# Moving the FFN weight loads from head 0 to head 3, and the gate matrix from eight DMA engines to four

## The chip, the cores and the metric

The kernel runs on one core of a Trainium2 chip. The metric is the device time of one execution in microseconds (us). Kernels are compared by the ratio to the runs of the kernel before taken in the same rounds on the same chip.

Three words are used throughout. A core's loads are carried out by sixteen *DMA engines*; a large load is cut into sixteen parts, and each part adds one to a semaphore when it has landed. A *packet* is one record of one DMA engine's work in the trace. *Delay* of an engine is how much later its last part landed than it would have with none of the extra work discussed here.

## The reference

A decode step for one token: layer norm of a row of 448 values, attention of 16 query heads over 8 cached heads of 65,536 keys of 256 values, and a small gated FFN, all added up. The cache is 512 MB in bf16 and each byte is used once; the FFN weights are three matrices of 1.6 MB.

```python
x = A_x;  xn = layernorm(x)
q = (xn @ wq)                         # 16 heads of 256
p = softmax(q @ k_cache^T / 16)       # 65536 keys in each of 8 cached heads
o = (p @ v_cache) @ wo
r = xn @ w_r
y = (silu(xn @ w_gate) * (xn @ w_up)) @ w_down
out = x + o + xn + y * sigmoid(r)     # one token: the top-1 choice is that token
```

## The kernel before

One queue (SyncE) issues all loads in a fixed order into a ring of buffers; an item is overwritten when TensorE has freed it. K and V items are 4 MB each, so every part is eight packets of 32 KB. V items of head h alternate with K items of head h+1.

```python
SPREAD = True

def flat_dma(src, n, off, spread):
    def d(a):
        dst = a[:, off:off + RP * n // 2]          # 128 partitions
        v = src.rearrange("a b -> (a b)")
        if spread:                                 # outer dim 8: eight DMA engines
            return dst, v.rearrange("(u a n) -> a u n", a=8, u=P // 8)
        return dst, v.rearrange("(p n) -> p n", p=P)
    return d
...
def v_next():
    ...
    kv_item(*v)
    if v[2] == 0 and v[3] == 2 * V_CHUNKS[0]:      # head 0, after its third V item
        item("ffn1", RP * F, [flat_dma(B_w_gate, F, 0, SPREAD), flat_dma(B_w_up, F, RP * F // 2, False)])
    if v[2] == 0 and v[3] == 3 * V_CHUNKS[0]:
        item("ffn2", FK * D, [... B_w_down ...])
...
def prog_sp():                                     # the queue that issues
    for n, it in enumerate(items):
        for m in range(max(0, it["need"] - 8), it["need"] + 1):
            wait("sp", "pe", ("FREE", m))
        for d in it["dmas"]:
            dst, src = d(ap_of(n))
            nc.sync.dma_start(dst, src).then_inc(sem_it[it["sem"]], 16)
```

In the regrouped view of the gate matrix, partition 16a+u of the buffer gets block 8u+a of the matrix (128 blocks of 12,544 bytes). TensorE's side gets a permuted copy of the input row for it, so the arithmetic is right either way. The up matrix is loaded plainly: partition p gets block p.

## Time and profile before

| | before |
|---|---|
| time | 1312.2 us (median) |
| bytes read, mean rate | 549 MB, 419 GB/s |
| PE busy | 70% |
| DMA share in the chain of waits | 73% |
| rate in a usual slice | 430 GB/s |
| rate in slices 5 and 6 (131 to 197 us) | 384 and 335 GB/s |

First the page of the kernel before: the parts with the span in 40 slices (DMA busy share in tenths, and what the engines moved), the queues, and the chain of waits.

```profile
DMA  9999999999999999999999999999999999999994
GB/s 400 430 430 430 384 335 433 431 427 432 431 430 429 429 430 429 431 429 431 431 431 431 428 430 430 431 430 429 428 430 429 431 423 430 430 430 431 431 430 205
...
q1 hardware_dynamic: 22026, 549.04, 98.5%
q8 instruction: 75, 1.23, 0.4%
q14 instruction: 12, 0.10, 0.0%
...
DMA 73%; PE 26%; another core or an unknown queue 1%; SPq 0%; issue 0%; DVE 0%
```

The engines never rest, and the rate is flat except for one dip. The dip is not idleness: the DMA share stays at 9. The windows view of the same kernel shows that (length, busy times, clock; the last two columns are DMA share and rate):

```profile
100.00:130.00 30.00, 27.56 (x304) 21.13 (x301) 20.38 (x36) 18.04 (x25) 0.00 (x0) 0.94 1.00 430
157.00:178.50 21.50, 8.88 (x112) 6.12 (x110) 5.66 (x9) 6.10 (x7) 0.00 (x0) 0.81 1.00 222
```

For 21.5 us sixteen busy engines moved 222 GB/s: 21.5 x (1 - 222/430) = 10.4 us were lost. In the packet records these are the very microseconds in which gate packets are in flight. A gate packet (12,544 bytes) takes about 0.94 us; a packet of the up matrix, of the same size, takes 0.47 us once the gate is done; K packets on engines without gate work take 2.38 us (median) instead of 1.21. This is called the *slow phase* below.

A load counts as landed only when its last part has. So the next thing to look at is how far apart the sixteen parts land. These three rows are worked out from the trace's semaphore records: when the first part of a load landed, and how much later each of the sixteen did, sorted. The records do not name the engines; which part belongs to which engine is inferred here and below from the order of the parts and its changes.

```
before, first part at   offsets of the sixteen parts (us)
 147.5 (before gate)    0.0 0.1 0.2 0.3 0.4 0.5 1.0 1.1 1.5 1.6 1.6 1.9 2.2 3.1 3.3 3.6
 191.0 (after gate)     0.0 0.5 1.2 1.3 2.0 2.7 2.8 2.8 7.3 7.4 7.7 7.8 8.6 9.7 10.6 11.0
1286.2 (last load)      0.0 0.4 3.7 4.0 4.0 4.2 6.8 9.6 9.7 9.8 9.9 10.5 10.6 11.4 19.2 19.5
```

(The last load of the queue is a piece of `wo`. The last V item, two loads before it, has the same offsets within 0.2 us.)

The gate opens a gap of 7 us between the eight engines that had it and the eight that had not. Between the second and the third row, eight engines fall back by about 9 us more: these carry the instruction fetches of queue 8, which go round eight engines in turn (75 packets of 16 KB, about 1.07 us each plus a slower neighbour packet). Two engines belong to both groups; they are 19 us behind at the end. The kernel ends 5 us after they do.

### The profile page before, as it was taken

Reading aid. Unit: us, or ns where it says so; the run is one execution under the profiler, and the core shown is the slowest. Engines: PE = TensorE matmul, PEld = TensorE weight load, DVE = VectorE, ACT = ScalarE, POOL = GpSimd, SP = SyncE. Lnnn points to the kernel's source line nnn. Section 1 sums busy time; section 2 is a strip of 40 time slices with the busy share of each in tenths; the row PEclk is TensorE's granted clock in tenths of the full one; section 3 lists DMA queues with packets and bytes.
Section 4 is the critical chain, followed back from the end, with each engine's and each line's share of the span. In section 5 each row is a group of like instructions: output and inputs, shape, how many; then the busy total and the mean of one; then the engine's idle time right before and its main releaser. Section 6 shows DMA issues by size and latency. Waiting matters only on the chain.

```text
span 1310.5 us, 20912 instructions
## 1 busy us (share of the span) xinstructions
PE 922.5 (70%) x9576; PEld 694.6 (53%) x9576; DVE 539.0 (41%) x895; ACT 432.4 (33%) x559; POOL 4.5 (0%) x34
## 2 busy tenths in 40 slices
PE   4998837768668577677677677577676686786534
PEld 4886625546546456455555556455465565565201
DVE  5776404444344344344343354344343353453200
ACT  2665303333233233233233243233332342332100
POOL 1000000000000000000000000000000000000000
PEclk9999768888888788787887888888887887888756
DMA  9999999999999999999999999999999999999994
GB/s 400 430 430 430 384 335 433 431 427 432 431 430 429 429 430 429 431 429 431 431 431 431 428 430 430 431 430 429 428 430 429 431 423 430 430 430 431 431 430 205
DMA packets 22117, 550.37 MB, mean 420 GB/s; under 512 B 2315, under 2 KB 4366, under 8 KB 4878
## 3 DMA queue, kind: packets, MB, share of 16 engines
q1 hardware_dynamic: 22026, 549.04, 98.5%
q8 instruction: 75, 1.23, 0.4%
q14 instruction: 12, 0.10, 0.0%
q10 hardware_dynamic: 4, 0.00, 0.0%
HBM read 549.03 MB, written 0.00 MB: 419 GB/s over the span
## 4 chain that ended last, share of the span: by engine, by line
DMA 73%; PE 26%; another core or an unknown queue 1%; SPq 0%; issue 0%; DVE 0%
DMA ring<-in_A_k_cache_dram 66%; PE ps_t L374 18%; DMA ring<-in_A_v_cache_dram 6%; PE ps_q L401 4%; PE ps_o L694 2%; PE ps_s L434 1%; PE ps_m L579 0%; SPq L304 0%; PE ps_m L644 0%; PE ps_s L562 0%; PE ps_m L534 0%; PE ps_m L505 0%; DVE ob_sb L514 0%; DVE res_bf L547 0%
## 5 line engine op out<-in xcount | busy, mean ns | idle before, releaser
L374 PE MATMUL ps_t<-ident_f,ring 128*128 128x128 f32 x4096 | 602.3, 310 | 302.1 <-DMA ring<-in_A_k_cache_dram 300.3
L374 PEld LDWEIGHTS ps_t<-ident_f,ring 128*128 128x128 f32 x4096 | 536.2, 161 | 419.1 <-DMA ring<-in_A_k_cache_dram 328.6
L358 DVE COPY kt_buf<-ps_t 128x1024 bf16<-128x1024 bf16 x768 | 492.6, 685 | 629.7 <-PE ps_t L374 628.7
L360 ACT ACTIVATE kt_buf<-ps_t 128x1024 bf16<-128x1024 bf16 x256 | 262.1, 1024 | 430.0 <-PE ps_t L374 429.2
L386 ACT ACTIVATE s<-ps_q 98x512 bf16<-98x512 f32 x256 | 152.9, 597 | 330.2 <-PE ps_q L401 330.2
L401 PE MATMUL ps_q<-kt_buf,qT_sb 128*2 128x512 bf16 x2048 | 173.5, 417 | 0.0
L694 PE MATMUL ps_o<-ring,S_sb 128*4 128x512 bf16 x2048 | 136.0, 410 | 48.9 <-DMA ring<-in_A_v_cache_dram 46.9
L694 PEld LDWEIGHTS ps_o<-ring,S_sb 128*4 128x4 bf16 x2048 | 50.7, 88 | 121.9 <-DMA ring<-in_A_v_cache_dram 54.9
L434 PEld LDWEIGHTS ps_s<-sel_bf,s 128*128 128x128 bf16 x1024 | 67.8, 102 | 7.6 <-ACT s L386 1.6
L434 PE MATMUL ps_s<-sel_bf,s 128*128 128x8 bf16 x1024 | 64.8, 169 | 0.7 <-ACT s L386 0.7
L514 DVE CAST ob_sb<-ps_o 100x512 bf16<-100x512 f32 x8 | 5.5, 692 | 83.2 <-PE ps_o L694 83.2
L401 PEld LDWEIGHTS ps_q<-kt_buf,qT_sb 128*2 128x2 bf16 x2048 | 26.3, 79 | 5.6 <-issue 0.2
L607 PE MATMUL ps_m<-xnT_sb,ring 128*128 128x2 bf16 x210 | 8.5, 179 | 18.0 <-DMA ring<-in_B_w_up_dram 16.4
L607 PEld LDWEIGHTS ps_m<-xnT_sb,ring 128*128 128x128 bf16 x210 | 8.4, 127 | 18.6 <-DMA ring<-in_B_w_up_dram 16.9
L480 ACT ACTIVATE S_sb<-S_sb,negmax 128x512 bf16<-128x512 bf16 x16 | 13.4, 863 | 5.3 <-DVE negmax L473 5.3
L414 DVE CAST S_sb<-ps_s 128x512 bf16<-128x512 f32 x16 | 10.9, 681 | 1.3 <-PE ps_s L434 1.3
L416 DVE TENSOR_REDUCE m1p<-S_sb 128x2 f32<-128x512 bf16 x16 | 11.0, 686 | 0.6
L592 DVE TENSOR_TENSOR gs_sb<-ps_m,sg_sb 128x14 f32<-128x14 f32 x1 | 0.2, 173 | 23.9 <-ACT sg_sb L587 23.9
L708 PE MATMUL ps_m<-ident_bf,xe_row 1*128 1x1 bf16 x16 | 0.6, 161 | 12.9 <-DVE xe_row L822 12.9
L505 PEld LDWEIGHTS ps_m<-rowsum,ones_f 128*128 128x128 f32 x32 | 5.5, 246 | 6.0 <-issue 6.0
L587 ACT ACTIVATE sg_sb<-ps_m 128x14 f32<-128x14 f32 x1 | 0.2, 184 | 22.2 <-PE ps_m L607 22.2
L708 PEld LDWEIGHTS ps_m<-ident_bf,xe_row 1*128 1x128 bf16 x16 | 0.5, 100 | 12.9 <-DVE xe_row L822 12.9
(67 smaller groups left out, 73.7 us busy)
## 6 DMA issues: line engine op xcount, KB each, us to landing
ring<-in_A_k_cache_dram SPq DMA_DIRECT2D x63, 4096.0 KB, 44.1
ring<-in_A_v_cache_dram SPq DMA_DIRECT2D x63, 4096.0 KB, 37.3
ring<-in_A_wq_dram SPq DMA_DIRECT2D x1, 3584.0 KB, 11.4
ring<-in_A_wo_dram SPq DMA_DIRECT2D x8, 448.0 KB, 29.2
ring<-in_A_k_cache_dram SPq DMA_DIRECT2D x2, 1024.0 KB, 13.4
ring<-in_A_k_cache_dram SPq DMA_DIRECT2D x1, 2048.0 KB, 20.6
ring<-in_A_v_cache_dram SPq DMA_DIRECT2D x1, 2048.0 KB, 41.6
ring<-in_B_w_gate_dram SPq DMA_DIRECT2D x1, 1568.0 KB
```

The lines of the kernel that those rows point to most:

```text
L358: op(e, ("EV", g), lambda x: x.tensor_copy(out=kt[:, :], in_=tb[:, :]))
L360: op(e, ("EV", g), lambda x: x.activation(out=kt[:, :], in_=tb[:, :], func=ACTF.Copy))
L374: ins = nc.tensor.matmul(ps_tf[g % NTB][:, jj * P:(jj + 1) * P], lhsT=kv[:, j + GN * m + jj, :], rhs=ident_f[:, :], is_transpose=True, sta ...
L386: op("act", ("EVQ", s), lambda e: e.activation(out=s2[s % 2][0:QROWS, :], in_=ps_q[0:QROWS, :], func=ACTF.Copy))
L401: ins = nc.tensor.matmul(ps_q[32 * m:32 * m + rep, 0:512], lhsT=qT_sb[:, hf, h * rep:(h + 1) * rep], rhs=kt[:, :].rearrange("p (k f) -> p ...
L414: op("dve", ("SCOPY", b), lambda e: e.tensor_copy(out=S[:, k * SBN:(k + 1) * SBN, :], in_=ps_s[:, :, :]))
L416: op("dve", ("SMAX", b), lambda e: e.tensor_reduce(out=m1p[:, h % 2, :, k], in_=S[:, k * SBN:(k + 1) * SBN, :].rearrange("p n i -> p i n") ...
L434: ins = nc.tensor.matmul(o, lhsT=s2[s % 2][:, jj * P:(jj + 1) * P], rhs=sel_bf[:, :, :], start=True, stop=True)
L480: op("act", ("EXPI", h, i), lambda e, i=i: e.activation(out=S[:, :, i], in_=S[:, :, i], func=ACTF.Exp, bias=negmax[:, h, i:i + 1], scale=1 ...
L505: ins = nc.tensor.matmul(ps_m[0:P, C_TOT + f * rep:C_TOT + (f + 1) * rep], lhsT=ones_f[:, :], rhs=rowsum[:, h, :], start=True, stop=True)
L607: ins = nc.tensor.matmul(o, lhsT=cols(a, rr * width, c), rhs=X[:, x0:x0 + 2], start=(b == 0), stop=(b == RP * half - 1), skip_group_check= ...
L694: ins = nc.tensor.matmul(ps_o[32 * g:32 * g + 2 * rep, :], lhsT=S[:, k:k + 2, :].rearrange("p n i -> p (n i)"), rhs=kv[:, j:j + 2, :], sta ...
```

## The change

Intent: place the FFN loads later, and keep the gate matrix off more of the DMA engines by giving it to the lowest four. ("At head h" means: issued among the V items of head h.) Cut to its core:

```diff
-SPREAD = True
+SPREAD = 4
+FFN_AT = 3
@@ flat_dma
-                return dst, v.rearrange("(u a n) -> a u n", a=8, u=P // 8)
+                return dst, v.rearrange("(u a n) -> a u n", a=spread, u=P // spread)
@@ v_next
-        if v[2] == 0 and v[3] == 2 * V_CHUNKS[0]:
-            item("ffn1", RP * F, [flat_dma(B_w_gate, F, 0, SPREAD), flat_dma(B_w_up, F, RP * F // 2, False)])
-        if v[2] == 0 and v[3] == 3 * V_CHUNKS[0]:
+        if v[2] == FFN_AT and v[3] == 2 * V_CHUNKS[0]:
+            item("ffn1", RP * F, [flat_dma(B_w_gate, F, 0, SPREAD), flat_dma(B_w_up, F, RP * F // 2, 0)])
+        if v[2] == FFN_AT and v[3] == 3 * V_CHUNKS[0]:
@@ dve_base: waits for RES of head FFN_AT - 1
@@ prog_dve: the permuted input row follows SPREAD
-        xv8 = xn_bf[0:1, :].rearrange("o (u a s) -> o a u s", s=RP, a=4)
+        xv8 = xn_bf[0:1, :].rearrange("o (u a s) -> o a u s", s=RP, a=SPREAD // 2)
```

Instruction counts and bytes are the same in both kernels.

## The prediction

> **What bounds it now.** Data transfer, in every stage. The page gives 420 GB/s, DMA share 9 of 9 in all slices but the last, PE busy 70%; the chain of waits is 73% DMA. By the windows view a normal stage moves 430 GB/s. So the time is set by the DMA engine that finishes last.
>
> The landings of each load's sixteen parts show that the engines are not level. Parts land within 3.6 us of each other at 147 us, within 11.0 us after the FFN loads (181 us), within 19.5 us at the end (1286.2 to 1305.7). Chaining packet records by start and end, I read the causes:
> - Instruction fetches (queue 8: 75 packets of 16 KB, about 1.07 us) go round eight engines. Each costs its engine about 1.5 us, 14 us per engine in all.
> - The gate matrix lies on eight engines, 16 packets of 12.5 KB each at about 0.94 us. Up packets of the same size take 0.47 us once the gate is done.
> - While any gate packet is in flight, all sixteen engines run at half speed: in the window 157 to 178.5 us, 222 GB/s with a DMA share of 1.00; 32 KB packets take about 2.4 us instead of 1.21. That is the 384 and 335 GB/s dip of the page: 10.6 us lost by everyone.
> - Delays come to about 11 us for an engine with neither load, 18 with gate only, 25 with fetches only, 33 with both. Two engines have both, and they end the kernel; six have the gate without these fetches (two of them with fetches of queue 14, up to 4 us).
>
> **What the change does.** Bytes, instructions and matmul counts stay. (1) The FFN loads move from head 0 to head 3, about 157 to about 630 us. DMA is the limit in both places, so this alone is worth about 0; the PE work stays hidden. (2) The gate goes over four engines, 32 packets each. The Trainium skill (DMA: Bandwidth & Descriptors, "Why a DMA increments its semaphore by 16 and not by 1") says a hardware-queue load on k engines uses the lowest-numbered k. The trace agrees so far: the small x load (one packet) ran on an engine that also had the gate, and that one shows no fetch of queue 8 up to the gate. I guess that the lowest four are free of these fetches.
>
> **Cost.** If a gate packet still takes 0.94 us and halves the rest, the slow phase is 30 us instead of 21. Delays (estimates): gate engines about 30, fetch engines 15 + 14 = 29, others 15. The last engine is at about 30 instead of 33: 3 us gained, on the critical path in full. Better balance (no engine with both loads) is mostly paid for by a slow phase half as long again.
>
> **Time: 1309 us**, range 1299 to 1322. Faster by over 2%: 0.02; within 2%: 0.96; slower by over 2%: 0.02.
>
> **Right if** the dip moves to about 610 to 660 us, is about 30 us long at about 220 GB/s and costs about 15 us; no dip near 160 us; the final spread shrinks from 19.5 to about 15 us, without two engines far behind the rest; the last V part lands about 3 us earlier.
>
> **Wrong if** one of the lowest four has the fetches of queue 8: its delay is 44 us and the kernel is some 10 us slower. If the queue-14 engines are among them, the gain is gone (+1). If more partitions per engine make the conflict worse (a third of the rate), +10 us; if four streams hurt the rest less than eight, the gain could be 10 to 14 us.

## The result and the profile after

The changed kernel took 1314.99 us (median of 4 runs, 1314.2 to 1315.3) against 1312.21. The ratio is 1.0025, with a 95% interval of 1.0007 to 1.0042: the same within 2%, but on the slow side, and so not the 3 us gained that the prediction named. (A ratio is the mean time of one kernel's runs over that of the other's in the same rounds, so not quite the ratio of the medians.) Executions over 1.5% slower than the fastest of the same kernel are left out of the means.

The page of the changed kernel, the lines that answer to those above:

```profile
DMA  9999999999999999999999999999999999999995
GB/s 400 431 430 430 429 431 431 430 430 429 431 431 427 429 430 431 427 430 429 259 420 409 429 430 431 429 432 426 430 431 431 429 430 430 429 432 430 430 430 227
...
DMA 69%; PE 28%; another core or an unknown queue 2%; SPq 0%; issue 0%; DVE 0%
```

And its windows: where the dip was, where it is now, and the stretch after it.

```profile
157.00:178.50 21.50, 15.80 (x166) 11.91 (x165) 9.33 (x16) 7.10 (x10) 0.00 (x0) 0.84 1.00 429
...
627.20:660.70 33.50, 13.65 (x139) 9.24 (x137) 7.74 (x12) 7.30 (x9) 0.00 (x0) 0.70 1.00 254
...
656.80:659.90 3.10, 0.00 (x0) 0.00 (x0) 0.00 (x0) 0.00 (x0) 0.00 (x0) 0.50 0.94 344
...
660.70:725.00 64.30, 43.38 (x490) 34.44 (x491) 23.31 (x38) 17.73 (x23) 0.00 (x0) 0.79 0.98 419
```

The dip has gone from 157 us and stands at 627 us: 33.5 us long, worth 33.5 x (1 - 254/430) = 13.7 us, near the 30 us and 15 us predicted. The third line is a part of the dip: from 656.8 to 659.9 us the packet records show one last engine with gate packets, and the rate was already back at 344 GB/s (see e5). The landings, again worked out from the trace:

```
after, first part at    offsets of the sixteen parts (us)
 617.2 (before gate)    0.0 0.2 0.2 0.3 0.3 0.4 2.4 3.9 6.1 6.1 7.8 7.8 7.9 7.9 8.4 8.4
 663.6 (after gate)     0.0 0.6 1.7 2.0 6.8 6.9 7.7 7.8 7.8 7.8 8.3 8.5 15.2 16.7 17.4 20.3
1292.5 (last load)      0.0 0.2 0.2 0.4 5.9 6.3 6.6 6.6 7.3 7.4 7.8 8.0 8.1 9.4 10.7 15.8
```

The first row shows three kinds of engine: six that carry no fetches, two a little behind (2.4 and 3.9 us), and eight with the fetches of queue 8. After the gate six engines have become four, the two in between have gone, and four are far back. So the lowest four are two engines of the first kind and both of the second. None of the lowest four has queue 8's fetches, as guessed. But one engine is alone at the end, 15.8 us behind, 5 us behind the next.

What slows the two in between? The trace has fetches of queue 14 at 750.3, 928.4, 929.5 and 1120.0 us. After the gate the last engine's offset rises exactly three times: from 13.2 to 14.1 across the first, from 14.1 to 15.0 across the middle pair (where the second last also rises, from 10.2 to 10.9), and from 15.1 to 16.0 across the last one. Both late engines carry queue 14, and the one that carries more of it ends the kernel. It landed at 1292.5 + 15.8 = 1308.3 us; the last engine of the kernel before landed at 1305.7 us.

One more thing in the trace looks like a cause and has to be tested: right after the dip the engines in front ran dry for about 7 us (the rate of 409 GB/s in slice 22). The changed kernel's waits of the issuing queue, for 600 to 740 us, put part of this down to the FFN matmuls that free the buffer late:

```profile
SPq L305 <- PE ps_s L435: 57.1, 4, 16.8
SPq L305 <- PE ps_m L608: 25.8, 1, 25.8
```

### The profile page after: what moved, and what is told of

It reads as the page before. It is cut to its first block, busy times and chain, and to the rows that moved or that the text cites. A ratio compares the mean times of both kernels' runs of the same rounds, so it can differ in the third digit from the quotient of the medians.

```text
span 1313.0 us, 20912 instructions
## 1 busy us (share of the span) xinstructions
PE 921.1 (70%) x9576; PEld 692.2 (53%) x9576; DVE 538.8 (41%) x895; ACT 432.2 (33%) x559; POOL 4.5 (0%) x34
## 3 DMA queue, kind: packets, MB, share of 16 engines
q8 instruction: 75, 1.23, 0.4%
## 4 chain that ended last, share of the span: by engine, by line
DMA 69%; PE 28%; another core or an unknown queue 2%; SPq 0%; issue 0%; DVE 0%
DMA ring<-in_A_k_cache_dram 60%; PE ps_t L375 19%; DMA ring<-in_A_v_cache_dram 9%; PE ps_q L402 5%; PE ps_o L695 2%; PE ps_s L435 1%; PE ps_m L608 0%; PE ps_m L580 0%; SPq L305 0%; PE ps_s L563 0%; PE ps_m L535 0%; DVE ob_sb L515 0%; DVE res_bf L548 0%; PE ps_m L466 0%
## 5 line engine op out<-in xcount | busy, mean ns | idle before, releaser
L415 DVE CAST S_sb<-ps_s 128x512 bf16<-128x512 f32 x16 | 10.9, 682 | 1.4 <-PE ps_s L435 1.4
```

Of the source, the lines that this page charges most:

```text
L415: op("dve", ("SCOPY", b), lambda e: e.tensor_copy(out=S[:, k * SBN:(k + 1) * SBN, :], in_=ps_s[:, :, :]))
```

## The experiments

The theory after the result had three parts. (a) The plain view costs nothing and the regrouped view makes all sixteen engines slow while it is in flight. (b) The time is set by the engine that is last in total, here a gate engine with queue 14. (c) The move alone is worth nothing. The rivals: that the move costs, because the ring of buffers is caught at a bad place; and that the slow phase comes from the FFN as such, from the small number of engines, or from the blocks that are read.

All edits are against the changed kernel. For values of SPREAD for which the permuted row would have no shape, `SPREAD // 2` became `(SPREAD or 8) // 2`.

### e1: only the move

```diff
-SPREAD = 4
+SPREAD = 8
```

> Only the move: gate over eight engines as before, but beside the values of head 3. Theory (the late engine is one that has the gate and queue-14 fetches, so the four-engine layout costs): no fourth-engine cost here, the two engines with fetches and gate are last again, 1312 to 1314 us, slow phase of 21 to 26 us near 630 us. Rival (the move costs, because the ring of buffers is caught at a worse place and engines run dry after it): 1315 us, as in the changed kernel.

Measured: 1315.9 us, ratio 1.0039 (1.0025 to 1.0052), 6 us slower than the kernel before. Part (c) of the theory falls. Time and slow phase were outside the theory's 1312 to 1314 us and 21 to 26 us, and the time is near the rival's 1315; e6 decides between the two. The windows view of e1:

```profile
627.20:657.80 30.60, 14.46 (x139) 9.35 (x137) 7.74 (x12) 7.42 (x9) 0.00 (x0) 0.72 1.00 226
```

The slow phase is 30.6 us instead of the 21.5 of the kernel before, for the same gate matrix over the same eight engines. The first landings row explains it: at 147 us the engines are 3.6 us apart, before the gate in e1 they are 8.7 us apart. The phase starts when the foremost gate engine gets to its gate packets and ends when the hindmost is done. The engine that is last spends the longer phase at half rate on its other packets too.

### e2: only the four engines

```diff
-FFN_AT = 3
+FFN_AT = 0
```

> Only the layout: gate over four engines, beside the values of head 0. Theory: slow phase of about 31 us at 157 us at half rate, last landing set by a gated engine with queue-14 fetches, 1314 to 1316 us. Rival (the move costs): 1312 us as before.

Measured: 1324.3 us, ratio 1.0107 (1.0094 to 1.0121). This is 14 us over the kernel before, where 2 to 4 had been expected. The direction fits neither rival alone: each half of the change costs, and both together (1.0025) cost less than either. The windows view of e2:

```profile
157.50:196.30 38.80, 7.38 (x97) 4.91 (x96) 4.76 (x8) 5.07 (x6) 0.00 (x0) 0.64 1.00 234
```

The slow phase has 38.8 us. In the packet records 56 packets of 12,544 bytes took over 1.05 us, up to 1.57; in the changed kernel none did. At head 0 the sixteen engines are nearly level (the six foremost within 0.4 us), at head 3 the four gate engines are up to 3.9 us apart. See e9.

### e3: the gate loaded plainly over sixteen engines

```diff
-SPREAD = 4
+SPREAD = 0
```

(In the matmuls the plain copy of the input row is then used, as for the up matrix.)

> Gate loaded as the up matrix is, over sixteen engines without a regrouped view, head 3. Theory: no slow phase at all, gate packets of 0.47 us; every engine carries 8 gate packets (3.8 us), the eight fetch engines end last at about 14 + 4 us of delay instead of 34 to 36: 1296 to 1298 us. Rival (the dip belongs to the FFN loads or their matmuls as such, not to the regrouped gate): a dip stays and the time is 1306 or more.

Measured: correct, 1297.8 us, ratio 0.9905 (0.9892 to 0.9919): it beats the kernel before by about 12 us and, by the ratios, the changed kernel by about 16. The page and the windows view of e3:

```profile
GB/s 404 428 429 431 429 432 431 427 433 426 432 430 426 435 429 428 433 427 429 429 431 429 428 433 428 431 432 424 432 432 428 432 427 432 432 426 433 431 426 253
...
626.40:642.30 15.90, 13.87 (x142) 10.51 (x140) 7.74 (x12) 7.71 (x9) 0.00 (x0) 0.84 1.01 428
```

There is no dip. All 256 packets of gate and up took 0.47 to 0.48 us. The same FFN matmuls run in the same place, so the dip did not belong to them. The last load, from e3's landings:

```
e3, first part at       offsets of the sixteen parts (us)
1275.6 (last load)      0.0 0.2 0.4 0.4 0.6 1.0 3.1 6.6 13.9 14.0 14.0 14.2 14.4 15.4 15.4 15.5
```

This row is what the fetches alone do: six engines level, two with queue 14 at 3.1 and 6.6, eight with queue 8 at 14 to 15.5.

### e4: sixteen engines, but the regrouped view

```diff
-SPREAD = 4
+SPREAD = 16
```

> Gate over sixteen engines, but with the same regrouped view as in the four- and eight-engine forms (16 groups of 8 partitions). If the halving comes from the regrouped view (which partitions an engine writes, or which blocks it reads): gate packets of 0.94 us and half rate for 8 to 17 us near 630 us, last engine at about 25 us of delay, 1302 to 1306 us. If it comes from using fewer than sixteen engines: no dip, 1296 to 1298 us.

Measured: 1309.2 us, ratio 0.9988 (0.9976 to 1.0001). Windows view of e4:

```profile
626.90:651.20 24.30, 15.08 (x141) 9.95 (x139) 7.74 (x12) 7.71 (x9) 0.00 (x0) 0.71 1.00 265
```

The halving is there with all sixteen engines at work, so it does not come from using fewer. The phase was longer than expected (24.3 us, not at most 17), because it lasts from the foremost to the hindmost engine, and so the time was 3 us above the expected range.

### e5: the same partitions written, other blocks read

```diff
-                return dst, v.rearrange("(u a n) -> a u n", a=spread, u=P // spread)
+                w = A_wq.rearrange("a b -> (a b)")[0:288 * RP * n // 2]
+                return dst, w.rearrange("(a u n) -> a u n", a=spread, u=288 // spread)[:, 0:P // spread, :]
```

with SPREAD = 8. Each engine now reads one contiguous stretch, of another matrix; the result is wrong. (Another matrix, because the gate matrix read in order was expected to be merged into the plain view by the compiler; no run shows that.)

> Wrong result on purpose. As e1 (eight engines, head 3), but the gate's 1.6 MB are read from another matrix so that each of the eight engines reads one contiguous stretch of 16 blocks, 450 KB from the next engine's; the partitions written are the same. If the halving comes from what is written (an engine writing groups of 16 neighbouring partitions, other engines' share): as e1, gate packets of 0.9 us, slow phase of 30 us at about 225 GB/s, 6 us over before. If it comes from the interleaved blocks that are read: packets of 0.47 us, no slow phase, about 21 us of delay for the last engine, 10 us under before.

Measured: 1316.9 us, ratio 1.0051 (1.0035 to 1.0068), as e1. Windows view of e5:

```profile
626.90:657.80 30.90, 14.33 (x141) 9.67 (x139) 7.74 (x12) 7.69 (x9) 0.00 (x0) 0.72 1.00 230
```

So it is not the interleaved reading. What e1, e2, e4 and e5 share, and e3 and the K, V and up loads lack, is how the 128 partitions written are dealt out to the engines. This fits two pages of the Trainium skill. "DMA: Bandwidth & Descriptors", section "The descriptor swizzle", says that in a plain transfer to 128 partitions each DMA engine writes the partitions of one port of its own. "SBUF — State Buffer", section "Door 1: The DMA port swizzle (why `[64,N]` ≈ `[32,N]`)", gives the partitions of each port: four neighbouring ones and the four that are 32 further on. By that table a group of 16 neighbouring partitions lies on four ports, and engines whose groups are 32 apart share theirs. The runs do not show the ports. No run gives the same view to partitions that are dealt out otherwise, so the form of the view itself stays as a rival. Three dimensions alone are not it: the view of `w_down` has three as well, with the partitions outermost, and its packets of 6,272 bytes took 0.24 us, the usual rate.

How many engines with such packets does it take? In the changed kernel the four parts of the gate landed at 653.7, 656.7, 657.8 and 660.8 us, about 1 us after their last packets, so one engine alone still had gate packets from 656.8 to 659.9 us. Of the 20 packets of 32 KB that started on the other engines from 657.3 to 659.9 us, 19 took 1.23 to 1.42 us, near the usual 1.21, and one took 1.95. The last 3.7 us of the gate in e10 (below) look the same:

```profile
972.20:975.90 3.70, 0.00 (x0) 0.00 (x0) 0.00 (x0) 0.00 (x0) 0.00 (x0) 0.50 0.95 370
```

Of the 34 packets of 32 KB that started there from 972.6 to 975.9 us, 32 took 1.22 to 1.38 us and two 1.88 and 2.34. So a single engine slows about one other at a time, which the sharing of a port could explain. Several at once bring all sixteen to about half rate, which is more than the table explains; why is left open.

### e6: the plain view at head 0

```diff
-SPREAD = 4
-FFN_AT = 3
+SPREAD = 0
+FFN_AT = 0
```

> Gate over sixteen engines in the plain view as in e3, but beside the values of head 0. Theory (the move costs only because the slow phase lasts until the last of the uneven engines has done its gate part): without a slow phase the place is worth nothing, same as e3 within 2 us, 0.990 of before. Rival (the place in the ring of buffers matters by itself): off e3 by 4 us or more.

Measured: 1298.1 us, ratio 0.9908 (0.9893 to 0.9923), against 0.9905 for e3. Without a slow phase these two places cost the same, so the place in the ring does not cost by itself. The rival of the move falls; what is left for the cost of e1 is the longer slow phase.

### e7: eight engines at head 5

```diff
-SPREAD = 4
-FFN_AT = 3
+SPREAD = 8
+FFN_AT = 5
```

> Gate over eight engines as before, still later, beside the values of head 5. Theory: the spread between the engines just before the load is about 11 us there (3.6 at head 0, 8.7 at head 3), so the slow phase is about 33 us (22 and 31) and the time 7 to 9 us over before (e1: 6). Rival (head 3 is a bad place of its own): back near before.

Measured: 1317.5 us, ratio 1.0055 (1.004 to 1.007), 7.8 us over. Windows view of e7:

```profile
940.40:976.00 35.60, 16.09 (x144) 10.97 (x144) 7.74 (x12) 7.71 (x9) 0.00 (x0) 0.71 1.00 230
```

The slow phase is 35.6 us, somewhat more than the 33 expected. With the eight-engine layout the phase grows with the distance between the engines: 21.8, 30.6 and 35.6 us at heads 0, 3 and 5 (counted from the first to the last packet of 12,544 bytes that took over 0.7 us).

### e8: two engines

```diff
-SPREAD = 4
+SPREAD = 2
```

> Gate over two engines, head 3: the suspected cost doubled. Theory: 64 packets an engine at 0.9 us, slow phase of about 58 us, all engines at half rate for that time; the last engine 60 us or more behind, 1338 to 1345 us. Rival (two streams disturb the rest less): packets near 0.5 us, at most 35 us, about 1315 us.

Measured: 1340.0 us, ratio 1.0228 (1.0213 to 1.0243). Windows view of e8:

```profile
628.60:686.00 57.40, 11.22 (x133) 7.80 (x131) 7.05 (x11) 6.67 (x8) 0.00 (x0) 0.62 1.00 259
690.00:740.00 50.00, 34.33 (x384) 27.52 (x388) 17.68 (x29) 12.90 (x17) 0.00 (x0) 0.75 0.70 289
```

Half as many engines, 1.7 times the slow phase, at the same rate. Just after it the last engine was 46.9 us behind the foremost, less than the 60 expected. The second line shows what happens when two engines are some 40 us behind: the others use up all that can be issued and idle (DMA share 0.70), because no buffer comes free before the last part of its item has landed.

### e9 and e10: four engines at heads 1 and 5

```diff
-FFN_AT = 3
+FFN_AT = 1        # e9; 5 in e10
```

> The changed kernel with its FFN loads beside head 1 instead of head 3. Theory of the +14 at head 0 (e2): there the four engines with the gate are level within 0.6 us, write to the same share of the partitions at once, and packets take up to 1.5 us. At head 1 the two engines with queue-14 fetches are 1.1 and 2.0 us behind the other two and from each other 1 us: fewer packets above 1.05 us than the 56 of e2, more than the 0 to 3 of the changed kernel, and a time between them, 1315 to 1321 us. Rival (head 0 is slow because the ring of buffers is not yet full ahead there): 1315 us or less, as in the changed kernel, with no packets above 1.05 us.

> The changed kernel with its FFN loads beside head 5. Theory: the four engines differ by about 6 us there (4 at head 3), so the slow phase grows by 1 to 2 us over the 33.5 of the changed kernel, and the last engine is again the one with most queue-14 fetches: 1314 to 1317 us. With eight engines the same move cost 2 us more.

Measured: e9 1318.7 us, ratio 1.0064 (1.0047 to 1.008), with 13 packets over 1.05 us; e10 1315.8 us, ratio 1.0041 (1.0026 to 1.0056), with a slow phase of 36.2 us (2.7 us longer than in the changed kernel, where 1 to 2 had been expected) and again one engine alone at the end. With four engines an early place is worse, and the number of packets above 1.05 us falls with the time: 56, 13, 0 and 1 at heads 0, 1, 3 and 5. That fits gate engines which are level and so meet at the same partitions' share, but this mechanism is argued from the counts; no run moves the engines apart alone.

## Why the prediction was right or wrong

The time of 1315.0 us lies in the range of 1299 to 1322 and the class "within 2%" is right. That says little for the mechanism: the range is 23 us wide and holds a gain as well as a loss. The 3 us gained are wrong in sign: it was 2.8 us lost. The landings allow the sum to be done engine by engine. e3 and e6 have no slow phase, so an engine's landing in them is its time with fetches and a plain gate; what the regrouped gate adds is read just after the phase, at the same item.

| engine that ends last | lands in e3/e6 | added by the gate | sum | measured |
|---|---|---|---|---|
| before: gate and queue 8 | 1291.8 | 202.0 - 188.0 = 14.0 | 1305.8 | 1305.7 |
| after: gate and queue 14 | 1282.2 | 683.9 - 657.8 = 26.1 | 1308.3 | 1308.3 |
| e1: gate and queue 8 | 1291.1 | 681.0 - 662.2 = 18.8 | 1309.9 | 1310.4 |
| e2: gate and queue 14 | 1282.3 | 220.5 - 184.6 = 35.9 | 1318.2 | 1317.3 |

(For each, the landing of that engine's part of the first item whose parts all landed after the slow phase, a V item, in the kernel named less that in e3 or e6. Since engines are told apart by the order of the parts alone, each sum is good to about 1 us.)

- **"The time is set by the DMA engine that finishes last": right.** The sums agree with the landings to within 1 us in all four kernels.
- **Slow phase of 30 us, 0.94 us a packet, 15 us lost: right** at head 3 (33.5 us and 13.7 us measured; 26.1 us added and the 3.8 us of the plain gate make 29.9 us for 32 packets, or 0.93 us each). "While any gate packet is in flight, all sixteen engines run at half speed" was too wide: with one engine left the rate was 344 GB/s, which is part of why the phase averaged 254 and not 220.
- **Fetch engines at 29, gate engines at 30: right for those without queue 14.** Counted from the foremost engine of e3 less its plain gate (1275.6 - 3.8 = 1271.8), the last fetch engine ends at 1300.7 - 1271.8 = 28.9, and the two gate engines with no fetches at 1300.5 - 1271.8 = 28.7 and 1301.9 - 1271.8 = 30.1.
- **"I guess that the lowest four are free of these fetches": right for queue 8, and the failing step.** The sum left out queue 14, which two of the lowest four carry. By the e3 row these fetches are worth 6.6 us on one of them, so the last engine was at 1308.3 - 1271.8 = 36.5 and not at 30. The prediction knew of these fetches ("up to 4 us"), had named the case and put it at +1; it was +2.6 at the landings. Had the four been free of both, the last landing would have been near 1301.9 us, that of the later gate engine with no fetches: a gain of about 4 (an estimate), close to the 3 predicted.
- **"(1) The move alone is worth about 0": wrong.** It cost 6 us with eight engines (e1), 7.8 at head 5 (e7). The prediction took the slow phase's length from the packets of one engine and left out that it lasts from the foremost engine's first to the hindmost's last. With four engines head 3 is better than head 0 (1.0025 against 1.0107, e2). So each half of the change costs more alone (6 and 14 us) than both together (3 us): they cannot be added. This error did not reach the predicted time, because the sum priced the four-engine gate as a whole, and that term was right (29.9 us for 30).
- **The engines that ran dry after the dip did not matter.** They were the foremost. In the changed kernel the last engine's parts of the two items around it landed at 726.5 and 736.1 us, 9.6 us apart, the normal pace of eight 32 KB packets (9.7 us).
- **The larger miss was what was not asked.** Both layouts are worse than the plain load. The trace before already had the number for it: 21.5 us at 222 GB/s next to up packets of 0.47 us.

## What to carry to other kernels

In a kernel whose DMA engines are always busy, ask which engine has the most work in total, and read it from when the parts of one load land, not from the mean rate; small things that sit on fixed engines, such as instruction fetches, add up there. Check the rate while a load with an unusual view is in flight: engines that are busy at half the rate look busy in every summary. A load that is meant to relieve some engines should first be compared with the plain load over all sixteen, which here won by 1% over the kernel before.

## What the Trainium skill lacked or had wrong

- "DMA: Bandwidth & Descriptors" (section "Why a DMA increments its semaphore by 16 and not by 1"): that a load on k engines uses the lowest-numbered k agrees with these runs as far as they go. The engine of the one-packet x load had the gate too, and fewer groups in the view gave more packets for each gate engine (16 with eight, 32 with four). The page does not say that a view which deals out neighbouring partitions in groups slows every engine of the core while several engines have such packets: 222 to 265 GB/s instead of 430 (before, e1, e4, e5), also with all sixteen engines (e4).
- "SBUF — State Buffer" (section "Door 1"): its port table says who would share a port, but not that several engines with such packets bring all sixteen to about half rate, while a single one leaves the others near the full rate (344 GB/s and 32 KB packets of 1.23 to 1.42 us, with one of 1.95, at the end of the changed kernel's dip).
- "Runtime: NRT & Kernel Launch" (section "Instruction fetch mechanics") describes refills in blocks of 16 KiB and calls their cost mostly hidden. The block size agrees for queue 8 (75 packets of 16,384 bytes); the fetches of queue 14 are packets of 8,192 bytes. What they cost the instruction streams was not measured here. The cost is not hidden from the DMA engines: about 14 us on each of eight engines by the end (e3), and these engines land last in the fastest version.
- No page that I found tells which DMA engines carry instruction fetches. Here, as far as the order of the landings tells, queue 8 used eight engines, two of them among the lowest eight and none among the lowest four; queue 14 used two of the lowest four.
